# Single remainder chunks on GpSimd, expert products gathered by kind, a new hand-written order, and constant products in TensorE's early gaps

## The chip, the core and the metric

The kernel runs on one core of a Trainium2 chip. The metric is the device time of one execution in microseconds (us), lower is better. Engines are named TensorE (PE, its weight loads PEld), VectorE (DVE), ScalarE (ACT), GpSimd (POOL) and SyncE (SP), which issues most transfers.

## The reference

Attention restricted to hash buckets, then a small expert layer on 128 chosen tokens of each batch:

```python
q_bits = (np.einsum('bhsd,dk->bhsk', q, proj) > 0)      # B, H, S, D = 4, 8, 768, 64; 6 bits
mask = q_bucket[:, :, :, None] == k_bucket[:, :, None, :]
scores = np.where(mask, scale * np.matmul(q, k.T), -1e9)
attn = softmax(scores);  x = attn @ v                    # x: (4, 768, 512)
scores = np.einsum('bsd,d->bs', x, w_gate)
top_idx = np.argpartition(-scores[b], 128)[:128]         # per batch
ye = np.maximum(x[b, top_idx] @ w1, 0.0) @ w2            # 512 -> 1024 -> 512
out[b, top_idx] = x[b, top_idx] + sigmoid(scores[b, top_idx])[:, None] * ye
```

## The kernel before, in words

The 32 heads (4 batches of 8) are worked through one after the other, several of them in flight. Values are split into high and low parts so that products keep float32 accuracy.

Preparation of a head: its queries and keys are loaded (X), a product with the projection gives the hash (`hash_half`, hp), VectorE turns it into signs (`signs`, sg), ScalarE and VectorE make the high and low parts XH and XL (`split_xh`, `split_xl`), and SyncE moves signs and parts into the operand tiles A (four) and B (two) (`place_signs`, `place_a`, `place_b`).

Row maxima: the hash bits decide a row's maximum, up to a shift. For this GpSimd subtracts one half of A's keys from the other (`k_diff`, tile kd). For each of six row tiles t TensorE makes two products of 384 columns, one with kd and one with A's second half (`max_unit`, tile mx); ScalarE takes the positive part of the first (`max_relu`, tile me, 2 buffers), VectorE adds the second and reduces (`max_red`, mj and m). The six maxima are turned by a product (`max_turn`, mt), copied (mr) and moved into A by SyncE.

Scores: nine units a head, each a bank of 512 columns (`st_unit`, tile st, 3 buffers); ScalarE takes the exponential (`st_exp`, tile P). A chunk is 128 keys by 768 queries; six a head, in three pairs. The value product takes P's bfloat16 high part and a float16 remainder R = P − high part. The remainder of pair 1 (chunks 2 and 3) was one operation on GpSimd (`r_pair`), the other four chunks one operation each on VectorE (`r_chunk`). `av` then makes, for a chunk, six times three products of 65 or 64 columns; the third of three needs R. `recip` and `norm` divide and store x.

GpSimd and VectorE are kept apart by hand at some places: `mine` notes VectorE's last operation of the kind that reads two tiles of SBUF, and `turn` makes a GpSimd operation wait for it.

The expert layer: `score` sums x times the gate, `choose` ranks the tokens of a batch (compare: cm; count: rp; selection: sel; token numbers: ip, idx) and gathers the rows with an indirect transfer from GpSimd (xe). `expert` splits them into three parts (xth, xtl, xtb), multiplies by w1's high part (two products) and low part (one bfloat16 product), four k tiles and two halves e; the hidden values are turned (ht), split and multiplied by w2 in eight k tiles the same way (yp). `apply_expert` serves batches 0 and 1, `apply_expert_fast` batch 2, `apply_expert_last` batch 3. `warm_last` makes eight products of w1 into an unused bank (wp); `warm(n)` makes n products of a constant 128 by 128 tile into a score bank (ws).

The order of all work is a list of words, ORDER, run in sequence: `s.3.4` is score unit 4 of head 3, `rd.3.1` a max reduction, `c0` the next piece of `choose(0)`, `e1` the next piece of `apply_expert(1)`, `wu.30` is `warm(30)`. An engine does its own instructions in this order. BANKS names the PSUM bank (of four) of each max, hash and expert tile in turn.

Of the kernel before, what the change touches and what calls it, by code (L numbers as in the profile page):

```python
# [41 lines left out]
ps.0.1 sg.0.1.1.2 ps.0.0 V.0 lc xl.0 pb.0.2 h.0.1.2.4 sg.0.1.2.4 xh.1 pa.1.1 xh.2 xl.1 h.0.0.2.4 sg.0.0.2.4  # L42
h.0.0.1.2 sg.0.0.1.2 ps.1.0 ps.1.1 pa.1.0 pb.0.3 ir.0 mx.0.0.1 kd.0 mx.0.0.0 re.0.0 rd.0.0 mx.0.1.1 mx.0.1.0
re.0.1 mx.0.2.0 pb.0.1 rd.0.1 re.0.2 mx.0.2.1 rd.0.2 mx.0.3.0 mx.0.4.0 mc re.0.3 w mx.0.3.1 ir.1 rd.0.3 re.0.4
mx.0.5.0 mx.0.5.1 mx.0.4.1 kd.1 mx.1.0.0 rd.0.4 mx.1.1.0 vh.0 re.0.5 rd.0.5 pb.0.0 vl.0 mt.0 mx.1.0.1 re.1.0
rd.1.0 mc2.0 mr.0 pa.2.1 pa.2.0 re.1.1 mx.1.1.1 rd.1.1 mx.1.2.0 re.1.2 mx.1.2.1 ia.2 rd.1.2 mx.1.3.0 pb.1.1
mx.1.3.1 pb.1.2 ps.2.1 sv.0 re.1.3 mx.1.4.0 xh.3 ps.2.0 pa.3.0 pb.1.3 re.1.4 w mx.1.5.1 w w rd.1.3 xl.2 X.5
mx.1.4.1 rd.1.4 mx.1.5.0 re.1.5 s.0.3 ia.3 e.0.3 s.0.6 e.0.6 s.0.5 e.0.5 s.0.0 e.0.0 rd.1.5 mt.1 mc2.1 sh.0
mr.1 kd.2 s.0.1 e.0.1 sl.0 s.0.2 mx.2.0.1 e.0.2 r.0.1 s.0.7 e.0.7 r.0.0 mx.2.0.0 re.2.0 s.0.4 rd.2.0 pb.1.0
e.0.4 X.4 V.1 rr.0.1 mx.2.1.0 re.2.1 mx.2.1.1 mx.2.2.0 s.0.8 X.6 mx.2.3.0 re.2.2 mx.2.2.1 rd.2.1 rd.2.2  # L50
mx.2.4.0 s.1.3 e.0.8 pa.3.1 re.2.4 re.2.3 s.1.5 X.7 e.1.3 e.1.5 vh.1 pb.2.0 mx.2.5.0 s.1.6 mx.2.4.1 mx.2.5.1
mx.2.3.1 xl.3 a.0.0 a.0.1 ps.3.0 ps.3.1 a.0.2 rd.2.3 r.0.4 e.1.6 a.0.3 r.0.5 a.0.4 a.0.5 re.2.5 xh.6 xh.4
s.1.0 rd.2.4 rd.2.5 pb.2.1 rc.0 n.0.0 h.1.0.0.4 s.1.2 h.1.1.0.4 pb.2.2 w w n.0.2 e.1.0 e.1.2 mt.2 mc2.2 mr.2
n.0.1 s.1.1 e.1.1 s.1.4 pb.2.3 pa.4.1 mx.3.1.1 e.1.4 pa.4.0 vl.1 s.1.8 kd.3 mx.3.1.0 sg.1.0.0.4 re.3.1
sg.1.1.0.4 mx.3.0.0 mx.3.0.1 re.3.0 rr.1.1 r.1.0 r.1.1 s.1.7 mx.3.2.0 a.1.0 a.1.1 ps.4.1 pb.3.2 pb.3.3 V.2
rd.3.0 rd.3.1 e.1.7 mx.3.3.0 ps.5.0 e.1.8 r.1.5 w ps.4.0 r.1.4 re.3.3 w w mx.3.3.1 mx.3.2.1 s.2.0 re.3.2 s.2.3
e.2.0 e.2.3 mx.3.4.0 s.2.5 e.2.5 a.1.2 a.1.3 w xl.4 sv.1 a.1.4 rd.3.2 pb.3.1 a.1.5 rd.3.3 xh.5 pa.5.1 rc.1
sh.1 mx.3.5.0 re.3.4 mx.3.4.1 rd.3.4 s.2.1 re.3.5 kd.4 sl.1 n.1.2 n.1.1 mx.3.5.1 rd.3.5 s.2.2 pb.3.0 e.2.1
s.2.4 mx.4.1.0 ps.5.1 e.2.2 mt.3 mc2.3 xl.5 mx.4.1.1 r.2.0 e.2.4 X.9 mx.4.0.0 s.2.6 mr.3 r.2.1 pa.5.0 re.4.1
mx.4.3.0 s.2.7 s.2.8 pb.4.1 pa.6.0 pb.4.0 pa.6.1 mx.4.0.1 rr.2.1 re.4.0 rd.4.0 rd.4.1 n.1.0 mx.4.2.0 w a.2.0  # L60
e.2.6 e.2.8 re.4.2 a.2.1 mx.4.2.1 rd.4.2 mx.4.4.0 re.4.3 pb.4.3 mx.4.3.1 e.2.7 s.3.3 vh.2 rd.4.3 e.3.3 s.3.6
e.3.6 mx.4.4.1 a.2.2 a.2.3 r.2.4 vl.2 mx.4.5.0 re.4.4 kd.5 re.4.5 s.3.8 rd.4.4 mx.4.5.1 pb.4.2 rd.4.5 s.3.5
# [24 lines left out]
xh.12 a.7.5 pb.9.0 rd.9.5 mt.9 s.8.8 xl.11 mc2.9 mr.9 w r.8.1 e.8.8 mx.10.2.0 rc.7 n.7.0 mx.10.1.0 s.8.3 e.8.3
n.7.1 sv.4 s.8.5 s.8.7 e.8.5 r.8.0 s.8.4 pb.10.2 pb.10.3 mx.10.0.0 sh.4 e.8.7 re.10.0 s.9.3 n.7.2 c0 s.9.0
sl.4 re.10.1 mx.10.1.1 e.9.3 pb.10.0 e.8.4 mx.10.0.1 rr.8.1 a.8.0 a.8.1 s.9.1 c0 c0 mx.10.2.1 rd.10.0 e.9.0
# [152 lines left out]
def body(ctx, tc, qk, v, pj, wg, w1, w2, cst, out):  # L242
# [330 lines left out]
    def r_chunk(h, c):  # L573
# [4 lines left out]
        ))  # L578
        st["rd", h, c] = True

    def r_pair(h, g):
        need(*(("e", h, 3 * g + i) for i in range(3)))
        pp = st["P", h, g]
        turn(nc.gpsimd.tensor_tensor(  # L584
# [512 lines left out]
```

## Time and profile before

| what | value |
|---|---|
| median of 3 runs | 464.59 us (461.87 to 466.11) |
| the profiled execution | 464.73 us, its span 463.0 us |
| mean granted TensorE clock | 0.967 |
| ScalarE's busy time | 342.6 us |
| GpSimd's busy time | 170.6 us |

The span runs from the first to the last instruction of the profile. Rows of the timeline give start, duration, engine, line and the tiles written and read; in square brackets stands the idle time of the engine ahead of the row and what ended it. A group's row gives count, busy time, mean duration in ns, and idle time ahead of it.

### The profile page before, as it was taken

The numbers are of one execution on the slowest core, as the hardware profiler recorded it, in microseconds if no ns is written. First come the engines' busy times: TensorE is split into PE (matmuls) and PEld (weight loads), VectorE is DVE, ScalarE is ACT, GpSimd is POOL, SyncE is SP. The second block draws the span as 40 slices with busy tenths as digits, with TensorE's granted clock in tenths as the row PEclk, the third lists the DMA queues.
The fourth block names the chain that finished last, engine by engine and source line by source line (L and its number), as shares of the span: only waits on it lengthen the run. The fifth ranks groups of instructions, "written<-read, shape, count | busy, mean of one in ns | idle before, by whom it ended". The sixth has DMA issues, their size and how long they took to land. (4 is left out here: it accounts for less than half of the span.)

```text
span 463.0 us, 14030 instructions
## 1 busy us (share of the span) xinstructions
PE 435.8 (94%) x5443; PEld 351.0 (76%) x5453; DVE 370.3 (80%) x890; ACT 342.6 (74%) x826; POOL 170.6 (37%) x109
## 2 busy tenths in 40 slices
PE   7899999999889899999989999999999989999995
PEld 4576877878766788888868878798788878887663
DVE  4756978788878998887897998898999988767721
ACT  2687889989857788888478877888878857855431
POOL 4363645554243355331423433515333223224010
PEclk9589999999898999999999998999999989999999
DMA  6786878867756656565763845687646245400210
GB/s 215 207 230 169 227 217 230 217 190 212 212 178 168 178 124 184 171 170 133 211 174 102 212 130 172 167 197 212 197 122 183 73 112 124 138 2 25 69 47 23
DMA packets 33222, 73.17 MB, mean 158 GB/s; under 512 B 5298, under 2 KB 11652, under 8 KB 33156
## 3 DMA queue, kind: packets, MB, share of 16 engines
q1 hardware_dynamic: 21732, 52.70, 43.5%
q10 hardware_dynamic: 10592, 17.44, 12.5%
q0 software_dynamic: 832, 2.13, 1.5%
q8 instruction: 43, 0.70, 0.7%
q14 instruction: 23, 0.19, 0.1%
HBM read 25.84 MB, written 7.35 MB: 72 GB/s over the span
## 5 line engine op out<-in xcount | busy, mean ns | idle before, releaser
L584 POOL TENSOR_TENSOR R<-P 128x1536 f16<-128x1536 f32 x32 | 93.7, 2929 | 136.0 <-ACT P L559 45.5
L512 DVE CUSTOM_DVE_ANT_0 mj<-mx,me 128x384 bf16<-128x384 f32 x192 | 106.2, 553 | 39.4 <-ACT me L504 15.1
L541 PE MATMUL st<-A 97*128 97x256 f32 (+1 forms) x384 | 132.2, 358 | 4.2 <-DMA A<-mr 3.9
L576 DVE TENSOR_TENSOR R<-P 128x768 f16<-128x768 f32 x128 | 127.8, 1028 | 5.2 <-ACT P L561 3.2
L545 PE MATMUL st<-B 128*128 128x256 f32 (+1 forms) x384 | 128.1, 347 | 0.0
L559 ACT ACTIVATE P<-st 128x512 f32<-128x512 f32 x192 | 111.7, 606 | 15.5 <-PE st L545 9.4
L504 ACT ACTIVATE me<-mx 128x384 f32<-128x384 f32 x192 | 92.4, 495 | 36.7 <-PE mx L496 19.3
L609 PEld LDWEIGHTS <-P 128*128 128x128 bf16 x2304 | 112.3, 98 | 7.0 <-issue 3.4
L609 PE MATMUL av<-V,P 128*128 128x65 f16 (+1 forms) x2304 | 117.6, 195 | 0.0
L609 PE MATMUL av<-V,R 128*128 128x65 f16 x1152 | 114.4, 193 | 0.9 <-DVE R L576 0.4
L609 PEld LDWEIGHTS <-R 128*128 128x128 f16 x1152 | 107.3, 100 | 1.5 <-DVE R L576 1.0
L541 PEld LDWEIGHTS st<-A 97*128 97x128 f32 x384 | 74.7, 194 | 14.4 <-ACT x L633 2.8
L545 PEld LDWEIGHTS st<-B 128*128 128x128 f32 x384 | 75.0, 195 | 3.4
L496 PE MATMUL mx<-kd,A 96*128 96x384 f32 x192 | 68.4, 388 | 5.4 <-DVE m L512 2.8
L496 PE MATMUL mx<-A 96*128 96x384 f32 x192 | 66.8, 380 | 2.6 <-DVE XL L387 1.8
L487 POOL TENSOR_TENSOR kd<-A 96x384 fp32r<-96x384 f32 x32 | 35.3, 1104 | 89.6 <-PE mx L496 28.5
L561 ACT ACTIVATE P<-st 128x512 f32<-128x512 f32 x96 | 57.4, 604 | 3.1 <-PE st L545 2.4
L633 ACT ACTIVATE x<-av,rc 128x64 f32<-128x64 f32 x192 | 46.5, 323 | 11.6 <-DVE rc L621 7.8
L496 PEld LDWEIGHTS mx<-kd,A 96*128 96x128 f32 x192 | 36.9, 199 | 16.3 <-DVE m L512 5.7
L496 PEld LDWEIGHTS mx<-A 96*128 96x128 f32 x192 | 37.8, 200 | 11.6 <-DVE XL L387 2.5
L387 DVE SCALAR_TENSOR_TENSOR XL<-X,XH 128x768 fp32r<-128x768 f32 x32 | 31.1, 971 | 0.3 <-issue 0.2
L382 ACT ACTIVATE XH<-X 128x768 fp32r<-128x768 f32 x32 | 27.0, 849 | 5.3 <-DMA A<-XH 5.2
(106 smaller groups left out, 449.9 us busy)
## 6 DMA issues: line engine op xcount, KB each, us to landing
A<-XH SPq DMA_DIRECT2D x64, 192.0 KB
B<-XL SPq DMA_DIRECT2D x64, 192.0 KB
B<-A SPq DMA_DIRECT2D x64, 192.0 KB
X<-in_qk_dram SPq DMA_DIRECT2D x31, 384.0 KB
V<-in_v_dram ACTq DMA_DIRECT2D x16, 384.0 KB
out_dram<-x ACTq DMA_DIRECT2D x8, 768.0 KB
W<-in_w_dram ACTq DMA_DIRECT2D x8, 512.0 KB
A<-sg SPq DMA_DIRECT2D x64, 18.0 KB
```

The source lines that it names most:

```text
L487: turn(nc.gpsimd.tensor_tensor(kd, a[0:96, 1, 0:384].bitcast(F32), a[0:96, 1, 384:768].bitcast(F32), op=ALU.subtract))
L496: nc.tensor.matmul(pt[:, :384], a[0:96, 0, t * P : (t + 1) * P], a[0:96, 1, 384:768] if i else st["kd", h], start=True, stop=True,)
L504: nc.scalar.activation(me, st["mx", h, t, 0][:, :384], AF.Relu)
L512: nc.vector.tensor_tensor_reduce(out=jk[:, :384], in0=st["mx", h, t, 1][:, :384], in1=st["me", h, t], op0=ALU.add, op1=ALU.max, scale=1.0, ...
L541: nc.tensor.matmul(pt[:, o : o + n], a[:, 1, c * P : (c + 1) * P], a[:, 0, q0 : q0 + n], start=True, stop=False,)
L545: nc.tensor.matmul(pt[:, o : o + n], bt[:, 1, c * P : (c + 1) * P], bt[:, 0, q0 : q0 + n], start=False, stop=True,)
L559: nc.scalar.activation(pp[:, r, 0:512], pt, AF.Exp, scale=ES)
L561: nc.scalar.activation(pp[:, :, 512:768], pt.rearrange("p (a b) -> p a b", a=2), AF.Exp, scale=ES)
L576: mine(nc.vector.tensor_tensor(r_tile(h, c // 2)[:, r], pp[:, r], hi_view(pp, r), op=ALU.subtract))
L584: turn(nc.gpsimd.tensor_tensor(r_tile(h, g), pp, pp.bitcast(BF16)[:, :, 1::2], op=ALU.subtract))
L609: nc.tensor.matmul(o[:, t, 0:n], l, vv[:, c, hh, v0 : v0 + n], start=False, stop=last and l is lo, skip_group_check=True,)
L633: nc.scalar.activation(x[:, t], o[:, t, 0:D], AF.Copy, scale=rc[:, t : t + 1])
```

## The change

Six things change together.

- Remainders: each chunk is an operation of its own, by the order list either on VectorE (`r_dve`, word r, 91 of them where 128 were) or on GpSimd (`r_pool`, word g, 101 where 32 pairs were).
- kd: on GpSimd (`kd_pool`, 18 heads) or on VectorE (`kd_dve`, word kv, 14 heads).
- The me tiles have three buffers where they had two.
- Expert products: the two products with a high part of the weights are made for each k, and the bfloat16 products with the low part are gathered, four in a row. In the last expert the parts of the second half are put in another sequence.
- Constant products: besides `wu.30` at the start there are twelve more such words (4, 8, 35, 46, 2, 3, 5, 2, 5, 2, 5 and 8 products, 125 in all), up to the first scores.
- ORDER and BANKS are new throughout.

```diff
+ME = 3
...
-X.1 X.0 X.2 X.3 i0 ia.0 ia.1 wu.30 h.0.0.0.1 h.0.1.1.2 xh.0 pa.0.1 pa.0.0 h.0.1.0.1 sg.0.0.0.1 sg.0.1.0.1
+i0 wu.30 X.1 xh.1 wu.4 h.0.0.1.2 h.0.1.1.2 X.0 X.3 X.2 lc ia.0 wu.8 h.0.0.0.1 sg.0.0.0.1 sg.0.0.1.2 h.0.1.0.1
...
-        kd = sb.tile([96, 384], F32R, tag="kd", name=f"kd{h}", bufs=1)
-        turn(nc.gpsimd.tensor_tensor(
-            kd, a[0:96, 1, 0:384].bitcast(F32), a[0:96, 1, 384:768].bitcast(F32), op=ALU.subtract
-        ))
...
+    def kd_pool(h):
+        turn(nc.gpsimd.tensor_tensor(**k_diff(h)))
+
+    def kd_dve(h):
+        mine(nc.vector.tensor_tensor(**k_diff(h)))
...
-        me = sb.tile([P, 384], F32, tag="me", name=f"me{h}_{t}", bufs=2)
+        me = sb.tile([P, 384], F32, tag="me", name=f"me{h}_{t}", bufs=ME)
...
-    def r_pair(h, g):
-        need(*(("e", h, 3 * g + i) for i in range(3)))
-        pp = st["P", h, g]
-        turn(nc.gpsimd.tensor_tensor(
-            r_tile(h, g), pp, pp.bitcast(BF16)[:, :, 1::2], op=ALU.subtract
-        ))
...
+    def rest(h, c):
         need(("e", h, 3 * (c // 2) + 2), ("e", h, 3 * (c // 2) + c % 2))
...
+    def r_dve(h, c):
+        mine(nc.vector.tensor_tensor(**rest(h, c)))
+
+    def r_pool(h, c):
+        turn(nc.gpsimd.tensor_tensor(**rest(h, c)))
...
+    def two(ks):
+        return [(k, i) for k in ks for i in (0, 1)]
+
+    def lows(ks):
+        return [(k, 2) for k in ks]
...
-                m.up(hp, e, (k,))
+                m.up(hp, e, two((k,)))
                 yield
+            m.up(hp, e, lows(range(4)))
+            yield
...
-        m.up(h1, 1, range(2), (0, 2, 1), True)
+        m.up(h1, 1, by_part(range(2), (0, 1, 2)))
...
-        m.up(h1, 1, range(2, 4), (0, 2, 1), True)
+        m.up(h1, 1, by_part(range(2, 4), (2, 0, 1)))
```

Three places show how instructions move. First TensorE's list between the last hash product of the first heads and the first max products; before:

```order
L358 MATMUL hp_0_2_180<-X_103,pjt 32x384
L358 MATMUL hp_0_1_184<-X_97,pjt 32x384
L496 MATMUL mx_0_1_193<-A_83 128x384
L496 MATMUL mx_0_0_197<-kd_195,A_83 128x384
L496 MATMUL mx_1_1_204<-A_83 128x384
```

and with the change (the first dots stand for the rest of 46 constant products, the second for one more):

```order
L362 MATMUL hp_1_2_228<-X_147,pjt 32x384
L307 LDWEIGHTS ones_75
L307 MATMUL ws_246<-ones_75 128x128
...
L505 MATMUL mx_0_0_293<-kd_244,A_83 128x384
L505 MATMUL mx_0_1_302<-A_83 128x384
L505 MATMUL mx_1_0_304<-kd_244,A_83 128x384
L505 MATMUL mx_3_0_310<-kd_244,A_83 128x384
L307 LDWEIGHTS ones_75
...
L505 MATMUL mx_1_1_317<-A_83 128x384
```

Constant products now stand ahead of the max products and among them, and the first max product is one with kd. Second GpSimd's list around heads 16 and 17 (R_0, R_1, R_2 are the three pairs of a head); before:

```order
L487 TENSOR_TENSOR kd_4440<-A_84 96x384
L584 TENSOR_TENSOR R_1_4474<-P_1_4383 128x1536
L487 TENSOR_TENSOR kd_4544<-A_85 96x384
L857 DMA out_dram<-ye_4546,idx_3350 3072x512
L584 TENSOR_TENSOR R_1_4892<-P_1_4742 128x1536
```

and with the change:

```order
L496 TENSOR_TENSOR kd_4719<-A_85 96x384
L592 TENSOR_TENSOR R_0_4899<-P_0_4700 128x768 x2
L592 TENSOR_TENSOR R_1_4970<-P_1_4897 128x768 x2
L592 TENSOR_TENSOR R_2_5051<-P_2_4985 128x768
L592 TENSOR_TENSOR R_0_5127<-P_0_5008 128x768 x2
L592 TENSOR_TENSOR R_1_5157<-P_1_5154 128x768
L592 TENSOR_TENSOR R_2_5211<-P_2_5017 128x768 x2
```

Where one pair stood for a head, five singles of head 16 (rows two to four) follow one another, some of them as a couple of one tile (x2); there are 20 such couples in the whole list, and at other heads fewer singles stand between two kd. Third TensorE's list where the rows of the last expert are turned (xp); before:

```order
L849 MATMUL yp_9077<-w2l,htb_8978 128x512
L777 MATMUL xp_9104<-cs,xe_9074 128x128 x4
L849 MATMUL yp_9077<-w2h,hth_8977 128x512
L849 MATMUL yp_9077<-w2h,B_87 128x512
L849 LDWEIGHTS htb_8978
L849 MATMUL yp_9077<-w2l,htb_8978 128x512
```

and with the change:

```order
L852 LDWEIGHTS htb_9145
L852 MATMUL yp_9188<-w2l,htb_9145 128x512
L782 MATMUL xp_9273<-cs,xe_9247 128x128 x4
L814 MATMUL mh_0_9289<-w1h,xth_9278 128x512 x4
L814 LDWEIGHTS xtb_9280
L814 MATMUL mh_0_9289<-w1l,xtb_9280 128x512
```

Before, six products of batch 2's expert stood behind the turned rows; now all of them stand ahead. The eight products of `warm_last` stood among the counts of batch 3 and are now TensorE's last.

More of the change, by code (lines that the diff above doesn't have):

```diff
@@ L46 @@
[L46 to L50, printed above, removed]
@@ L803, in gate2, with up @@
             nc.vector.reciprocal(ss[:, 1:2], ss[:, 1:2])
-        def up(hp, e, ks, order=(0, 1, 2), by_part=False):
-            ki = [(k, i) for k in ks for i in order]
-            if by_part:
-                ki = [(k, i) for i in order for k in ks]
-            for k, i in ki:
+        def up(hp, e, kis):
+            done = t.get(("u", e), 0)
+            for k, i in kis:
                 l, r = t["x"][i]
@@ L812, in up @@
                     hp, l[:, k * P : (k + 1) * P], r[:, k, e * 512 : e * 512 + 512],
-                    start=(k == 0 and i == order[0]), stop=(k == 3 and i == order[-1]),
+                    start=done == 0, stop=done == 11,
                 )
+                done += 1
+            t["u", e] = done
         def relu(hp, e):
@@ L841, in split_h2, with down @@
             nc.vector.tensor_tensor(hl[:, f], tp, hh[:, f].bitcast(F32), op=ALU.subtract)
-        def down(yp, ks, order=(0, 1, 2), by_part=False):
-            ki = [(k, i) for k in ks for i in order]
-            if by_part:
-                ki = [(k, i) for i in order for k in ks]
-            for k, i in ki:
+        def down(yp, kis):
+            done = t.get("d", 0)
+            for k, i in kis:
                 l, r = t["h"][i]
@@ L850, in down @@
                     yp, l[:, k * P : (k + 1) * P], r[:, k],
-                    start=(k == 0 and i == order[0]), stop=(k == 7 and i == order[-1]),
+                    start=done == 0, stop=done == 23,
                 )
+                done += 1
+            t["d"] = done
         def finish(yp):
@@ L883, in st_bank, with by_part @@
         return pst.tile([P, 512], F32, tag="st", name=name)
+    def two(ks):
+        return [(k, i) for k in ks for i in (0, 1)]
+    def lows(ks):
+        return [(k, 2) for k in ks]
+    def by_part(ks, order=(0, 2, 1)):
+        return [(k, i) for i in order for k in ks]
     def apply_expert(b):
@@ L910, in apply_expert @@
         for k in range(8):
-            m.down(yp, (k,))
+            m.down(yp, two((k,)))
             yield
+            if k % 4 == 3:
+                m.down(yp, lows(range(k - 3, k + 1)))
+                yield
         yield
@@ L924, in apply_expert_fast @@
         for k in range(4):
-            m.up(h0, 0, (k,))
+            m.up(h0, 0, two((k,)))
             yield
+        m.up(h0, 0, lows(range(4)))
+        yield
         m.relu(h0, 0)
@@ L929, in apply_expert_fast @@
         for k in range(2):
-            m.up(h1, 1, (k,))
+            m.up(h1, 1, two((k,)))
             yield
@@ L937, in apply_expert_fast @@
         for k in range(2, 4):
-            m.up(h1, 1, (k,))
+            m.up(h1, 1, two((k,)))
             yield
+        m.up(h1, 1, lows(range(4)))
+        yield
         m.relu(h1, 1)
@@ L942, in apply_expert_fast @@
         for k in range(2):
-            m.down(yp, (k,))
+            m.down(yp, two((k,)))
             yield
@@ L949, in apply_expert_fast @@
         for k in range(2, 8):
-            m.down(yp, (k,))
+            if k == 4:
+                m.down(yp, lows(range(4)))
+                yield
+            m.down(yp, two((k,)))
             yield
+        m.down(yp, lows(range(4, 8)))
+        yield
         m.finish(yp)
```

371 lines of the change are left out of this document (189 added, 182 removed), and 10 rows, old and new, of the table BANKS.

## The prediction

> **What bounds the kernel now.** First the page: its shares of busy time, and the row of the granted clock.
>
> ```profile
> span 463.0 us, 14030 instructions
> PE 435.8 (94%) x5443; PEld 351.0 (76%) x5453; DVE 370.3 (80%) x890; ACT 342.6 (74%) x826; POOL 170.6 (37%) x109
> PEclk9589999999898999999999998999999989999999
> ```
>
> TensorE is the engine to follow, VectorE the next. The clock row dips in its second and third slice and in a few later ones. The view by stretches shows the start, the body and two of the later dips:
>
> ```profile
> 0.00:11.70 11.70, 8.20 (x46) 4.67 (x46) 5.57 (x9) 3.39 (x4) 5.33 (x14) 1.00 0.66 215
> 12.33:25.98 13.65, 12.75 (x43) 8.60 (x44) 9.32 (x31) 9.22 (x19) 6.11 (x9) 0.50 0.76 193
> 26.00:427.00 401.00, 384.56 (x5177) 318.03 (x5183) 340.09 (x804) 318.43 (x780) 155.54 (x85) 0.98 0.61 164
> 138.60:142.00 3.40, 3.40 (x19) 1.45 (x21) 2.37 (x4) 3.23 (x10) 1.61 (x1) 0.50 0.19 40
> 374.10:377.50 3.40, 3.40 (x70) 3.40 (x67) 3.17 (x7) 1.93 (x4) 1.00 (x1) 0.51 0.73 205
> ```
>
> (Columns: length, then TensorE, its weight loads, VectorE, ScalarE, GpSimd, then the granted clock, DMA share and GB/s.) At the start TensorE runs at half clock for 13.65 us. Five short stretches of the body look like the last two rows.
>
> A busy TensorE is not one at its peak. The starts of its products in the timeline show how dense they can stand:
>
> ```profile
> 409.26 0.28 PE L541 MATMUL st<-A 97*128 97x256 f32 x1
> 409.38 0.28 PE L545 MATMUL st<-B 128*128 128x256 f32 x1
> 409.50 0.34 PE L496 MATMUL mx<-kd,A 96*128 96x384 f32 x1
> 409.68 0.34 PE L496 MATMUL mx<-A 96*128 96x384 f32 x1
> 409.86 0.39 PE L849 MATMUL yp<-w2h,hth 128*128 128x512 f32 x1
> 410.09 0.40 PE L849 MATMUL yp<-w2h,htl 128*128 128x512 f32 x1
> 426.05 0.22 PE L609 MATMUL av<-V,P 128*128 128x65 f16 x2
> 426.14 0.22 PE L609 MATMUL av<-V,P 128*128 128x65 f16 x2
> ```
>
> A 256-column product takes 0.12 us, 384 columns 0.18, 512 columns 0.23, and three value products 0.09. By the code there are 768 score products (half of 512 columns, half of 256), 384 max products and 3456 value products; they need 134, 69 and 104 us so, together 307. The experts' 192 products add 44. With hashes, sums and transposes I estimate 390 us of the 463. So some 70 us are waits and lost clock, and those a new order can reach. What the waits are, these rows show:
>
> ```profile
> 272.92 2.75 POOL L584 TENSOR_TENSOR R<-P 128x1536 f16<-128x1536 f32 x1 [2.90 <-ACT P L559]
> 273.25 2.79 DVE L740 TENSOR_SCALAR sel<-iota,rank 128x128 f16<-128x128 f16 x3
> 276.57 0.67 PE L745 MATMUL ip<-tok,sel 128*128 128x1 f16 x6 [1.07 <-DVE m L512]
> 133.77 1.07 POOL L487 TENSOR_TENSOR kd<-A 96x384 fp32r<-96x384 f32 x1 [3.61 <-PE mx L496]
> 133.89 3.02 DVE L576 TENSOR_TENSOR R<-P 128x768 f16<-128x768 f32 x1
> 134.81 1.28 POOL L670 TENSOR_TENSOR w2l<-W,w2h 128x512 bf16<-128x512 f32 x1
> 138.38 0.22 PE L521 MATMUL mt<-identr,m 128*6 128x128 f32 x1 [2.24 <-DVE m L512]
> 368.81 2.71 DVE L740 TENSOR_SCALAR sel<-iota,rank 128x128 f16<-128x128 f16 x3
> ```
>
> While GpSimd works on its pair of chunks (272.92 to 275.67), VectorE's small sel operations stretch to 2.79 us: the two engines exclude each other. Behind them wait the max reductions, TensorE's max banks stay full, and TensorE idles 1.07 us. At 133.89 a chunk on VectorE takes 3.02 us, through two GpSimd operations in a row, and TensorE idles 2.24 us. There are five holds of over 2 us (the first at 133.89, the last at 368.81), and after four of them follows one of the half-clock stretches.
>
> **The change part by part.** The prices of one operation, from the views of the lines and the page's groups:
>
> ```profile
> L576 DVE TENSOR_TENSOR R<-P x128: 917/952/3020, 28.7 to 425.6; 128x768 f16<-128x768 f32 x128
> L584 POOL TENSOR_TENSOR R<-P x32: 2746/2843/3333, 30.6 to 421.5; 128x1536 f16<-128x1536 f32 x32
> L487 POOL TENSOR_TENSOR kd<-A x32: 989/1012/1823, 11.6 to 392.7; 96x384 fp32r<-96x384 f32 x32
> L670 POOL TENSOR_TENSOR w1l<-W,w1h x8: 1277/1286/1874, 23.7 to 83.1; 128x512 bf16<-128x512 f32 x8
> L375 DVE TENSOR_SCALAR sg<-hp 128x384 fp32r<-128x384 f32 x14 | 7.3, 550 | 0.2 <-PE hp L358 0.2
> ```
>
> *The start.* Here stand what TensorE's 30 constant products took, the hash products (two records each, so 8 in 4.82 us) and the first max product:
>
> ```profile
> 1.01 3.38 PE L303 MATMUL ws<-ones 128*128 128x128 f16 x30 [1.01 <-POOL ones L284]
> 5.07 4.82 PE L358 MATMUL hp<-X,pjt 128*32 128x384 f32 x16 [0.68 <-DMA X<-in_qk_dram]
> 11.74 0.41 PE L496 MATMUL mx<-A 96*128 96x384 f32 x1 [1.84 <-DVE XL L387]
> ```
>
> Added are 125 such products, 93 ahead of the first max product and 32 between the max products of heads 0 and 1. At 0.11 us each (3.38 over 30) the 93 cost 10 us, at twice that rate 5; idle TensorE time before 11.7 us is 3.5 (11.70 less 8.20). They are not wholly covered. Head 1's two hash products (0.6 each) and twelve of the constants also come ahead of head 0's hash, so head 0's signs, which SyncE moves, land about 2.3 us later (1.2 and some 1.1). I therefore set the first max product 2.3 us later, with the last block of 46 just filling the wait. Its kd now comes from VectorE (0.55 there, by the sg row of as many elements, against 1.0 on GpSimd). That is a new wait on VectorE for the moved signs; behind it queue the XL of head 0 and the first max reductions, which free TensorE's max banks and the me buffers. In return the clock should stay full: it fell at 12.33, behind the idle 1.84, which now holds products. At full clock TensorE's 12.75 us in that stretch shrink to about 6.4 and VectorE's 9.32 bind, which saves 13.65 − 9.3 = 4.3. Net −2.0. Ends: −4.3 if nothing is late; +5.8 if the clock falls all the same and the 32 cost 3.5 more.
>
> *Single chunks.* VectorE loses 37 of 128 chunks (37 × 0.952 = 35.2 us) and gains 14 kd (14 × 0.55 = 7.7): 27.5 us less. GpSimd gets 101 singles for 32 pairs and 18 kd for 32. No row has a single: it is at least half a pair, 1.37, and at most 1.93 (the 512-element w1l by 768/512). I take 1.45, near half the pair, since operation and types are the same. GpSimd then works 146 on chunks against 93.7, in all near 210 of 463, still with room. A hold lasts at most 1.45 us instead of 2.75, unless singles stand in a row, and 20 couples do (rows with x2). Five holds cost 5 × 1.65 us idle (the mean of 1.07 and 2.24) and four half-clock stretches 4 × 1.7 (half of 3.4): 15.1 us. I take half of it: −7.5. Ends: −15.1, and +12 if four more holds come than go.
>
> *New order, a third buffer for me.* The waits view names the couple which a third buffer loosens:
>
> ```profile
> DVE mj L512 <- ACT me L504: 15.1, 24, 2.8
> ACT me L504 <- DVE m L512: 14.6, 16, 2.5
> ```
>
> These are idle times of VectorE and ScalarE, and only their trace in TensorE counts. In the body TensorE idles 401 − 384.6 = 16.4 us by the stretch row, part of it already in the holds. With VectorE 27.5 us lighter I take a quarter: −4.0. Ends: −16.4 (all), and +8 (half the idle time of now once more), where value products wait for a chunk that GpSimd does late. A single waits for its own chunk's exponentials and for VectorE's last operation on the shared side, no longer for the whole pair; but on GpSimd's queue it stands behind earlier singles, kd and the weights' low parts, and the gathers of the experts' rows stand behind it. SyncE's list keeps its 329 rows; only their order moves.
>
> *Gathered expert products.*
>
> ```profile
> 410.79 0.40 PE L849 MATMUL yp<-w2h,htl 128*128 128x512 f32 x1
> 445.50 1.28 PE L811 MATMUL mh<-w1h,xth 128*128 128x512 f32 x4
> 448.41 0.62 PE L811 MATMUL mh<-w1h,xth 128*128 128x512 f32 x2
> ```
>
> Mixed by threes, a period is 410.09 to 410.79: 0.233 each. Gathered, as the last expert has it already, twelve take 445.50 to 448.41: 0.243 each. I take 0, with ends −1.0 and +1.5 for 144 products.
>
> *The tail.*
>
> ```profile
> 439.72 0.97 POOL L755 DMA_INDIRECT xe<-out_dram,idx x1 [13.17 <-DVE idx L1031]
> 444.50 0.59 ACT L784 CAST xth<-xp 128x512 fp32r<-128x512 f32 x1 [2.04 <-PE xp L777]
> ```
>
> The last expert waits for its gather (439.72) and then for xth, ready at 445.09; its products start at 445.50 behind six of the expert before. These now come earlier, and the eight warming products move from ahead of them to the very end, beside the closing transfer: −0.4, ends −0.4 and +1.3 (the six not done in time).
>
> Sum: −2.0 − 7.5 − 4.0 + 0 − 0.4 = −13.9. The profiled execution took 464.73 us, 1.7 beyond its span and 0.14 over the median of the runs (464.59): 464.7 − 13.9 = **450.8 us**.
>
> **The rivals.** *Holds by chains (slower).* The row at 133.89 shows a hold through two GpSimd operations. With the 20 couples, and up to five of six chunks of heads 16 and 17 on GpSimd, holds near 2.9 us can become more frequent than the five of now. Each costs 3.0 (15.1 / 5). Against −6.4 from the other terms, nine such holds make it slower: 464.7 − 6.4 + 4 × 3.0 = 470.3; with ten 473.3. Against it: most singles stand apart.
>
> *Holds vanish (faster still).* If a held VectorE operation goes in as soon as the running GpSimd operation ends, no hold exceeds 1.45 us and all 15.1 go; with 12 of the 16.4 us of idle: 464.7 − 2.0 − 15.1 − 12 − 0.4 = 435.2. The row at 133.89 speaks against it, the pairs (one operation, one hold) leave it open. The Trainium skill, page "SBUF — State Buffer", section "SBUF: two separate sides", says that the shared port pair is locked for one whole instruction and that the loser blocks fully; by that the holds end with each single. The trace agrees for the pair at 272.92 (held until 275.67) and not for the two at 133.77 and 134.81.
>
> *Nothing moves.* The order before already hides VectorE, and the holds only change places: A start of −2.0 and −0.4 leave 462.3. For it: TensorE's floor of 390 us does not move at all.
>
> **How the numbers follow.** Forecast 0.48 (442 to 459), holds vanish 0.21, nothing moves 0.17, chains 0.14. A measurement of this kernel tells about 1% (4.6 us) from no change. Faster by over 1% are the first two, 0.69; within 1% 0.17; slower 0.14. The range runs from 437, inside the second case, to 468, which leaves out the worse chains: 437 to 468. The ends of the terms together (427 and over 490) are wider, but would need all to fall one way.
>
> **What would show it.** Right: a granted clock of 1.00 from 12 to 26 us and first scores before 24 us; VectorE near 340 us busy, GpSimd near 210; a single at 1.4 to 1.5 us; no VectorE chunk above 2.4 us; at most two half-clock stretches in the body. Wrong: chunks held 2.9 us behind couples of singles, idle TensorE before value products with GpSimd's R as releaser, or a first max product after 15 us.

## The result, and the profile after

The changed kernel took 466.32 us (median of 20 runs, 463.49 to 471.42), the kernel before 461.96 beside it (20 runs, 459.14 to 469.24): a ratio of 1.0101, 95% interval 1.0069 to 1.0132. It is slower by 1.0%, some 4.4 us; forecast were 13.9 us less. Ratios, here and below, compare each kernel's faster executions alone, so that they can differ from the ratio of two medians. The profiled execution of the changed kernel took 465.07 us; that of before, 464.73, lies 2.8 us above the median that 20 runs give, which is why the two spans hardly differ.

From the page of the changed kernel: the span, the busy times, the granted clock, GpSimd's chunks.

```profile
span 463.2 us, 14366 instructions
PE 439.2 (95%) x5578; PEld 357.6 (77%) x5578; DVE 353.7 (76%) x867; ACT 344.2 (74%) x826; POOL 221.6 (48%) x164
PEclk9999999999999997999998999999989999999999
L592 POOL TENSOR_TENSOR R<-P 128x768 f16<-128x768 f32 x101 | 159.6, 1593 | 136.7 <-DVE R L589 40.9
```

And its stretches, cut as in the prediction:

```profile
0.00:11.70 11.70, 10.70 (x89) 7.10 (x91) 4.37 (x7) 2.97 (x3) 7.79 (x18) 1.00 0.81 254
12.33:25.98 13.65, 13.06 (x121) 9.15 (x119) 10.08 (x32) 8.83 (x18) 5.83 (x6) 1.00 0.51 132
26.00:427.00 401.00, 383.40 (x5157) 319.20 (x5155) 323.48 (x783) 321.31 (x781) 203.49 (x136) 0.98 0.63 166
```

The clock stays at 1.00 through the start, as meant, and VectorE is 16.6 us lighter. Neither shortens the kernel: in the body TensorE is busy 383.4 us of 401, where it was 384.6. What the start gives to the first max product is seen in the timelines, here the kernel before (SyncE's move of head 0's signs, GpSimd's kd, ScalarE's load of the first weights) and then the changed kernel:

```profile
8.42 1.57 SPq L394 DMA_DIRECT2D A<-sg  x2
11.64 0.99 POOL L487 TENSOR_TENSOR kd<-A 96x384 fp32r<-96x384 f32 x1 [5.52 <-DVE XL L387]
15.64 0.36 ACTq L657 DMA_DIRECT2D W<-in_w_dram  x1
```

```profile
6.01 0.46 ACTq L662 DMA_DIRECT2D W<-in_w_dram  x1
8.57 2.17 DVE L379 TENSOR_SCALAR sg<-hp 32x384 fp32r<-32x384 f32 x4 [6.08 <-PE hp L362]
10.77 2.88 SPq L398 DMA_DIRECT2D A<-sg  x3
15.04 0.55 DVE L499 TENSOR_TENSOR kd<-A 96x384 fp32r<-96x384 f32 x1 [1.19 <-DMA A<-sg]
15.65 0.45 PE L505 MATMUL mx<-kd,A 96*128 96x384 f32 x1 [0.32 <-DVE kd L499]
```

The signs leave 2.4 us later and then need 4.3 us to land instead of at most 3.2; the first max product comes at 15.65 instead of 11.74. Of these 3.9 us, 1.8 are left at the first scores (25.46 instead of 23.64). The holds of the body have other faces than before. Two places of the changed kernel (score sums jks, GpSimd's chunks, TensorE's max products):

```profile
238.98 3.89 POOL L592 TENSOR_TENSOR R<-P 128x768 f16<-128x768 f32 x2 [2.79 <-ACT P L570]
239.71 1.83 DVE L652 CUSTOM_DVE_ANT_0 jks<-x,wgt 128x512 bf16<-128x512 f32 x1
241.58 1.83 DVE L652 CUSTOM_DVE_ANT_0 jks<-x,wgt 128x512 bf16<-128x512 f32 x1
244.81 0.44 PE L505 MATMUL mx<-kd,A 96*128 96x384 f32 x1 [1.82 <-DVE sg L379]
...
338.66 1.01 POOL L496 TENSOR_TENSOR kd<-A 96x384 fp32r<-96x384 f32 x1 [5.21 <-PE mx L505]
338.76 2.89 DVE L652 CUSTOM_DVE_ANT_0 jks<-x,wgt 128x512 bf16<-128x512 f32 x1
339.63 1.46 POOL L592 TENSOR_TENSOR R<-P 128x768 f16<-128x768 f32 x1
```

A score sum takes 0.69 when nothing is in its way. The group's mean, before and after:

```profile
L647 DVE CUSTOM_DVE_ANT_0 jks<-x,wgt 128x512 bf16<-128x512 f32 x18 | 13.1, 728 | 1.8
```

```profile
L652 DVE CUSTOM_DVE_ANT_0 jks<-x,wgt 128x512 bf16<-128x512 f32 x18 | 18.5, 1026 | 1.6
```

Over all operations of VectorE that a GpSimd operation overlapped, the time beyond the usual one of their form (its first quartile, where the excess is over 0.1 us) adds to some 25 us before and some 32 after. Holds of over 2 us beyond the usual time fell from five to two (61.65 and 338.76); the smaller ones became more.

### The profile page after: what moved, and what is told of

Its sections match the earlier page's. It is cut to its first block, busy times and chain, and to the rows that moved or that the text cites. A ratio compares the mean times of both kernels' runs of the same rounds, so it can differ in the third digit from the quotient of the medians.

```text
span 463.2 us, 14366 instructions
## 1 busy us (share of the span) xinstructions
PE 439.2 (95%) x5578; PEld 357.6 (77%) x5578; DVE 353.7 (76%) x867; ACT 344.2 (74%) x826; POOL 221.6 (48%) x164
## 5 line engine op out<-in xcount | busy, mean ns | idle before, releaser
L592 POOL TENSOR_TENSOR R<-P 128x768 f16<-128x768 f32 x101 | 159.6, 1593 | 136.7 <-DVE R L589 40.9
L550 PE MATMUL st<-A 97*128 97x256 f32 (+1 forms) x384 | 130.4, 354 | 2.9 <-DMA A<-mr 2.9
L554 PE MATMUL st<-B 128*128 128x256 f32 (+1 forms) x384 | 126.2, 344 | 0.0
L614 PE MATMUL av<-V,P 128*128 128x65 f16 (+1 forms) x2304 | 120.1, 195 | 0.0
L614 PE MATMUL av<-V,R 128*128 128x65 f16 x1152 | 116.2, 193 | 0.7 <-POOL R L592 0.2
L589 DVE TENSOR_TENSOR R<-P 128x768 f16<-128x768 f32 x91 | 94.0, 1055 | 6.0 <-ACT P L570 4.0
L505 PE MATMUL mx<-kd,A 96*128 96x384 f32 x192 | 64.3, 366 | 4.3 <-DVE m L521 1.9
L505 PEld LDWEIGHTS mx<-A 96*128 96x128 f32 x192 | 36.1, 193 | 10.5 <-DVE m L521 4.3
L496 POOL TENSOR_TENSOR kd<-A 96x384 fp32r<-96x384 f32 x18 | 20.1, 1116 | 44.9 <-PE mx L505 12.2
L391 DVE SCALAR_TENSOR_TENSOR XL<-X,XH 128x768 fp32r<-128x768 f32 x32 | 34.6, 1084 | 1.5 <-ACT XH L386 1.5
```

Of the source, the lines that this page charges most:

```text
L391: mine(nc.vector.scalar_tensor_tensor(xl, st["X", h], XS, st["XH", h].bitcast(F32), op0=ALU.mult, op1=ALU.subtract))
L505: nc.tensor.matmul(pt[:, :384], a[0:96, 0, t * P : (t + 1) * P], a[0:96, 1, 384:768] if i else st["kd", h], start=True, stop=True,)
L550: nc.tensor.matmul(pt[:, o : o + n], a[:, 1, c * P : (c + 1) * P], a[:, 0, q0 : q0 + n], start=True, stop=False,)
L554: nc.tensor.matmul(pt[:, o : o + n], bt[:, 1, c * P : (c + 1) * P], bt[:, 0, q0 : q0 + n], start=False, stop=True,)
L589: mine(nc.vector.tensor_tensor(**rest(h, c)))
L592: turn(nc.gpsimd.tensor_tensor(**rest(h, c)))
```

## The experiments

Each line: median of 6 to 12 executions, and ratio to the kernel before run beside it on the same chip, with its 95% interval. The kernel before took 462.2 to 463.7 in these.

| run | what | median us | ratio to before |
|---|---|---|---|
| a_nowu | changed, without the 125 added products | 466.49 | 1.0115 (1.0065 to 1.0164) |
| a_start | changed, start of before | 462.18 | 1.0011 (0.9974 to 1.0048) |
| b_start | before, changed start | 466.86 | 1.0091 (1.0048 to 1.0134) |
| b_split | before, pairs as two singles | 460.37 | 0.9973 (0.9932 to 1.0015) |
| a_sg | changed, head 0's signs first | 468.93 | 1.0148 (1.0089 to 1.0207) |
| a_e0late | changed, first expert's start later | 466.03 | 1.0099 (1.0064 to 1.0133) |
| a_sel | changed, sel and jks in the hand-made order | 455.31 | 0.9882 (0.9822 to 0.9942) |
| b_me3gath | before, third me buffer, gathered products | 462.26 | 1.0004 (0.9966 to 1.0042) |
| a_w | changed, first weights' load late | 465.99 | 1.0069 (1.0032 to 1.0106) |
| a_w_lc | the same, constants late too | 468.66 | 1.0112 (1.0060 to 1.0164) |
| a_w_sel | a_w and a_sel | 454.15 | 0.9818 (0.9771 to 0.9866) |
| b_sel | before, sel and jks in the hand-made order | 456.62 | 0.9874 (0.9833 to 0.9916) |
| a_sg_w | a_sg and a_w | 464.78 | 1.0055 (1.0010 to 1.0099) |
| a_start_sel | a_start and a_sel | 453.48 | 0.9848 (0.9781 to 0.9915) |
| b_split_sel | b_split and b_sel | 459.89 | 0.9969 (0.9929 to 1.0010) |
| a_jks | a_sel with jks alone | 459.33 | 0.9896 (0.9818 to 0.9975) |
| a_all | a_sel, a_sg and a_w | 452.59 | 0.9785 (0.9733 to 0.9837) |
| a_all_gather | a_all, first gather let through | 450.21 | 0.9732 (0.9672 to 0.9791) |

### Start and body apart

The order is a list of words, so one kernel's first words can stand in front of the other's rest. b_start takes the changed order up to its last `wu` word (116 words) and then the words of before that are still missing; a_start the first 97 words of before and then the rest of the changed ones. BANKS follows its tiles. a_nowu only drops words; b_split splits the pair:

```diff
-        turn(nc.gpsimd.tensor_tensor(
-            r_tile(h, g), pp, pp.bitcast(BF16)[:, :, 1::2], op=ALU.subtract
-        ))
+        for r in range(2):
+            turn(nc.gpsimd.tensor_tensor(
+                r_tile(h, g)[:, r], pp[:, r], hi_view(pp, r), op=ALU.subtract
+            ))
```

> The changed kernel without the 125 added constant products (only the first 30 stay); nothing else differs. Theory 'start': the added products keep the granted clock at 1.00 from 12 to 26 us, but the first max product moved from 11.74 to 15.65 us, and that delay is paid to the end; without them the first max product comes before 14 us again, the clock dips to about 0.5 somewhere before 26 us, and the time is 2 to 4 us below the changed kernel's (near 463). Theory 'holds': the loss lies in the body, where GpSimd's singles hold VectorE for 31.8 us in all against 24.7 before; then the time stays within 1 us of the changed kernel's 466.3, or rises by the half clock.

> The changed kernel with the order of before for its first 97 words (hashes, signs and max products of heads 0 and 1 up to the end of the added products, kd of head 0 on GpSimd, no added products), and its own order from there. Theory 'start': the first max product near 11.7 us, half clock from 12 to 26 us as before, first scores near 23.6, and the time 2 to 4 us below the changed kernel's 466.3. Theory 'holds': within 1 us of 466.3.

> The kernel before with the first 116 words of the changed order (all added constant products, kd of head 0 on VectorE), and its own order behind them. Theory 'start': 2 to 4 us slower than before (464 to 466). Theory 'holds', with my forecast's term for the start: 1 to 3 us faster than before (459 to 461), with the clock at 1.00 from 12 to 26 us.

> The kernel before with each of its 32 pairs on GpSimd as two single chunks in a row at the same place; nothing else differs. A single takes 1.46 us by the changed kernel's rows, two of them 2.9 where the pair took 2.75. Theory 'holds': what holds VectorE is the time GpSimd works, not the length of one operation, so VectorE's operations are held as long as before or longer and the time is the same or up to 3 us more (462 to 465). My forecast's term: a held operation goes in between the two singles, no hold is over 1.5 us, and the time falls by 3 us or more (below 459). Theory 'start' says nothing of it.

a_start and b_start agree: the start alone costs 4 us, the whole loss, and the rest of the change nothing that can be told. The added products are not to blame: without them (a_nowu) the time is the same and the first max product still late, at 15.31 us, now with half clock. In b_start the clock did not stay full, it fell to half for 3.4 us at 19.7 and again at 26.5 us. In b_split neither theory is shown, the time is within the interval of no change. Its trace shows why so little comes of the singles where the selections stand; here GpSimd's pair, VectorE's sel and TensorE's max products in the kernel before, and then the same place with two singles in b_split:

```profile
157.71 2.75 POOL L584 TENSOR_TENSOR R<-P 128x1536 f16<-128x1536 f32 x1 [5.10 <-ACT P L559]
158.13 2.71 DVE L740 TENSOR_SCALAR sel<-iota,rank 128x128 f16<-128x128 f16 x3
161.37 0.62 PE L496 MATMUL mx<-kd,A 96*128 96x384 f32 x2 [1.16 <-DVE m L512]
```

```profile
156.07 2.89 POOL L585 TENSOR_TENSOR R<-P 128x768 f16<-128x768 f32 x2 [5.09 <-ACT P L559]
156.49 2.69 DVE L741 TENSOR_SCALAR sel<-iota,rank 128x128 f16<-128x128 f16 x3
159.71 0.61 PE L496 MATMUL mx<-kd,A 96*128 96x384 f32 x2 [1.05 <-DVE m L512]
```

The first sel (1.10 us) ends when the first single does, at 157.5, and the second (1.50 us) when the second does, at 159.0. By the pair three sel took 2.71 us and TensorE idled 1.16; with two singles it is 2.69 and 1.05. The Trainium skill, page "SBUF — State Buffer", section "SBUF: two separate sides", says that the engine which starts first has the shared ports for its whole instruction and the other is blocked. Here the trace agrees, but between two singles only one small operation goes in, and the next single holds the next one, so the sum stays what GpSimd works.

### The start

Words moved (a_sg: head 1's hash and signs behind head 0's; a_w: the first `w`; a_w_lc: also `lc` and `mc`):

```diff
-wu.4 h.0.0.1.2 h.0.1.1.2 X.0 X.3 X.2 lc ia.0 wu.8 h.0.0.0.1 sg.0.0.0.1 sg.0.0.1.2 h.0.1.0.1
+wu.4 X.0 X.3 X.2 lc ia.0 wu.8 h.0.0.0.1 sg.0.0.0.1 h.0.1.0.1 h.0.0.1.2 h.0.1.1.2
-xh.0 pa.0.1 ir.1 sg.0.1.1.2 pa.0.0 sg.0.1.0.1 ps.0.1 ia.1 ps.0.0 wu.35
+xh.0 pa.0.1 ir.1 sg.0.1.0.1 pa.0.0 ps.0.1 ia.1 ps.0.0 sg.0.0.1.2 sg.0.1.1.2 wu.35
```

```diff
-ps.1.0 sg.0.1.2.4 pa.1.0 w mc pb.0.0 kv.0 wu.46
+ps.1.0 sg.0.1.2.4 pa.1.0 mc pb.0.0 kv.0 wu.46
-mx.0.4.0 re.0.3 re.0.2
+mx.0.4.0 re.0.3 w re.0.2
```

> The changed kernel with one thing reordered in the start: head 0's two hash products and its signs come ahead of head 1's on TensorE, VectorE and in SyncE's list (as in the kernel before); the 125 added products, their places and kd on VectorE stay. Theory 'signs': what costs the start 4 us is that head 0's signs leave 2.4 us later (10.77 us instead of 8.42) because head 1's are made ahead of them; then here the first max product comes at 13 to 14 us instead of 15.65, and the time falls by 1.5 to 3.5 us (463 to 465), with the clock still at 1.00. Rival 'products in the way': TensorE, filled by the added products, is late itself; then the first max product stays after 15 us and the time at 466.

> The changed kernel with its first word w (ScalarE's queue then issues the 512 KB load of the first weights at 6.01 us) moved behind the fourth max step of head 0, where the kernel before has it (issued at 15.64); nothing else differs. Theory 'transfers': head 0's signs are small, but they land late because of the large transfers issued ahead of them: 3.2 us from issue (8.42) to GpSimd's kd (11.64) before, 4.3 us in the changed kernel (10.77 to 15.04), 6.2 without the added products (8.50 to 14.70) and 7.9 with head 0's signs first (8.49 to 16.44), so that making the signs earlier did not help. With the load late, kd starts 2 to 3 us earlier, the first max product comes before 14 us, and the time falls by 2 to 4 us (462 to 464). Rival 'SyncE's list': the signs wait for SyncE's own transfers (X, constants, XH); then nothing changes (466).

> As the run before, with the 259.5 KB load of the constants (lc, issued by SyncE at 2.61 us, 10.03 in the kernel before) and the copies made of it (mc) moved to the places of before too. Theory 'transfers': a further 0.5 to 1.5 us earlier than with the weights alone, first max product at 12 to 13 us, 461 to 463. Rival 'SyncE's list': the whole gain comes only here, 3 to 4 us below the changed kernel, and none in the run before.

> The changed kernel with both edits of the start: head 0's hash and signs ahead of head 1's, and the first weights' load late. Alone the first made it slower (signs issued at 8.49 us but landed at 16.44) and the second gained 1.6 us by its trace (signs issued at 10.05, kd at 13.04 with no wait). Theory 'two delays in a row' (signs made late, and transfers in their way, each hiding the other): kd near 11.5 us, first max product at 12 to 13, first scores near 22.5, 2 to 4 us below the changed kernel (462 to 464). Rival: the queue of transfers is full anyway (V, the constants, X of heads 2 and 3), and the signs land after 14 us again: no faster than with the late load alone (466).

My theory of the signs fell with a_sg, which was not faster (468.93). Its move of the signs and its kd, then those of a_w and of a_sg_w:

```profile
8.49 2.35 SPq L398 DMA_DIRECT2D A<-sg  x3
16.44 0.55 DVE L499 TENSOR_TENSOR kd<-A 96x384 fp32r<-96x384 f32 x1 [4.30 <-DMA A<-sg]
```

```profile
10.05 2.52 SPq L398 DMA_DIRECT2D A<-sg  x3
13.04 0.55 DVE L499 TENSOR_TENSOR kd<-A 96x384 fp32r<-96x384 f32 x1
```

```profile
8.31 2.99 SPq L398 DMA_DIRECT2D A<-sg  x3
12.29 0.55 DVE L499 TENSOR_TENSOR kd<-A 96x384 fp32r<-96x384 f32 x1
```

In a_sg the signs leave 2.3 us earlier than in the changed kernel and land 1.4 later: issued 2.5 us behind the 512 KB of weights (5.97 there), they take 7.9 us. TensorE stands 3.4 us for them, and half clock comes back for 13.65 us (from 16.7). With the weights late, kd has no wait for the signs: they land within 3.0 us in a_w and 4.0 in a_sg_w. So two delays stood in a row: the first max product comes at 14.41 in a_w and 13.66 in a_sg_w, the first scores at 24.19 and 23.44 (25.46 in the changed kernel). The gain, by the ratios some 1.5 and 2 us, is short of what I expected or at its low end, and not clear of the noise: the intervals overlap that of the changed kernel. About half of the 4 us of the start stays open: the move of before was issued at 7.27 in a_start, and head 0's hash began at 5.13 where a_sg_w has 5.59.

a_w_lc is not faster than a_w, against both theories; by the medians it is 2.7 us slower, though the intervals overlap. VectorE's copies of the constants now stand among the first max reductions, where GpSimd works:

```profile
16.57 1.00 POOL L496 TENSOR_TENSOR kd<-A 96x384 fp32r<-96x384 f32 x1 [7.63 <-DVE m L521]
16.60 1.06 DVE L323 CAST iota<-cs 128x128 f16<-128x128 f32 x1
17.52 1.45 POOL L294 MEMSET A<- 32x1536 f32 x1
17.58 1.42 DVE L324 CAST tok<-cs 128x6 f16<-128x6 f32 x1
```

Copies of 0.22 and 0.17 us take 1.06 and 1.42: a hold again, through a subtraction and a memset, and half clock behind it (18.7 to 25.5).

### The held small operations

R, XL and cm stood in `mine` (and kd, where VectorE makes it), sel and jks did not, although jks reads two tiles of SBUF. a_sel, b_sel and the runs built on them wrap both; a_jks has the second hunk only:

```diff
-            nc.vector.tensor_scalar(sel[:, t], iota16, rank[:, t : t + 1], None, op0=ALU.is_equal)
+            mine(nc.vector.tensor_scalar(sel[:, t], iota16, rank[:, t : t + 1], None, op0=ALU.is_equal))
-            nc.vector.tensor_tensor_reduce(
+            mine(nc.vector.tensor_tensor_reduce(
                 out=jk[:, : d1 - d0], in0=x[:, t, d0:d1], in1=wgt[:, d0:d1],
...
-            )
+            ))
```

> The changed kernel in which VectorE's selections and score sums (sel, jks) also count for the hand-made order of the two engines: a GpSimd operation that stands behind them in the list waits until they are done. Nothing else differs. Theory 'holds': the held small operations (sel 1.2 us each, jks up to 2.2 us) cost TensorE some 1 to 2 us each, about 10 us over the ranking stretches; with fewer of them held the time falls by 2 us or more (464 or less). Rival 'holds are cheap': GpSimd's chunk only starts later and value products wait for it instead; within 1 us of 466.3, or slower.

> The changed kernel with only jks (the score sums) in the hand-made order, sel as it was. By the traces, heads 16 and 24, where jks stood held (three of 1.1 to 2.2 us at 239.71, 241.58 and 338.76), gained 7.6 of the 10.6 us, and the stretch at 279, where sel was held, some 1.3. Theory 'jks first': 456 to 459. Rival 'sel first' (sel stands in the chain of ranking, gather and expert): 461 or more.

> The kernel before (pairs on GpSimd, its own order) with sel and jks in the hand-made order of the two engines. Theory 'holds': the pairs' holds of sel (2.1 to 2.2 us at 158.13, 273.25 and 368.81) go, with the half-clock stretches behind them, 4 to 9 us faster than before (454 to 459), so what I expected of the single chunks was to be had from the order of the two engines alone. Rival: a pair that waits for the selections is late for its value products; within 2 us of before.

> The kernel before with its pairs as two single chunks each, and sel and jks in the hand-made order. With pairs that order gave 456.6; two sel holds of 2.1 and 2.3 us were left (152.90, 265.57), where the pair stood ahead of sel in the list. If single chunks are worth something once the small operations are kept apart, as my forecast of the holds had it, these two holds shrink and the time is 2 us or more below 456.6. Rival: two singles in a row hold as long as a pair; within 1.5 us of 456.6.

> The kernel before with three buffers for me instead of two, and with the gathered expert products in batches 0 to 2; order and all else as before. My forecast gave the gathered products nothing and the third buffer a share of 4 us together with the new order. Theory 'the max stage is not the bound': within 1 us of before. Rival: the third buffer alone loosens the waits of VectorE and ScalarE on each other (15.1 and 14.6 us idle), 2 us or more faster than before.

a_sel is 11 us faster than the changed kernel (10 by the ratios), far more than I expected. The same place as above, in a_sel, and the stretch from 236 to 249.5 us in the changed kernel and in a_sel:

```profile
238.97 0.69 DVE L652 CUSTOM_DVE_ANT_0 jks<-x,wgt 128x512 bf16<-128x512 f32 x1
239.81 3.48 POOL L592 TENSOR_TENSOR R<-P 128x768 f16<-128x768 f32 x2 [5.10 <-DVE sc L652]
```

```profile
236.00:249.50 13.50, 11.68 (x112) 9.28 (x112) 12.09 (x27) 9.99 (x23) 5.91 (x5) 0.87 0.54 151
```

```profile
236.00:249.50 13.50, 13.43 (x182) 11.30 (x179) 10.30 (x29) 12.05 (x30) 8.73 (x6) 1.00 0.55 160
```

GpSimd waits 5.10 us for the last score sum, all six of which take 0.69, and nothing waits for its chunk: TensorE fills the stretch, at full clock. By the ends of the heads' value products in the two traces, 1.7 us are won by head 12 (sel), 3.4 at head 16 (the score sums above), 1.3 by head 20 (sel) and 4.2 at head 24 (score sums). Held time fell from some 32 to 24 us. a_jks alone gets some 7 of the 11 us by the medians and 9 of the 10 by the ratios, and its interval holds a_sel's 0.9882: the score sums are most of it, and that the selections count too is seen in the traces only. V's split, not kept apart either, was held for 3.49 us in the kernel before (236.26); no run wraps it.

b_sel shows that the stake was there before the change, and needed none of it: 1.3% from two wrapped calls. The gain, some 5.8 us, lies within the 4 to 9 expected. b_split_sel is not faster than b_sel but slower, 0.9969 against 0.9874: the singles are not worth anything once jks is kept apart, and its sel are held as in b_split (by 1.04 and 1.26 us at 271). Held time is some 3 us longer than in b_sel; whether that is its whole loss is not shown. Buffers and gathered products (b_me3gath) give nothing that can be told, as expected.

### The first gather

a_e0late moves the first two `e0` words behind `mx.14.0.1` and `n.11.1`. a_all_gather moves `rd.13.0 rd.13.1` from behind `a.11.3` to ahead of `r.11.2`.

> The changed kernel with the first two pieces of the first expert (its transposes, gate and splits) moved some 30 words later, behind two products of head 14's maxima; nothing else differs. In the changed kernel the gather of its rows took 4.57 us on GpSimd (163.73 to 168.30, where 1.48 before), while VectorE ran kd, R, V and two R in a row from 163.37 to 167.38; TensorE then stood 3.5 us at 171.33 and ran at half clock for 6.8 us (3.3 us lost). Theory 'gather': that stall is a loss of the new order; with the pieces later the stall of 3.5 us goes, and with it most of the half clock: 3 to 6 us faster than the changed kernel (460 to 463). Rival: only the place of the wait changes, since ScalarE and VectorE have other work that was late there; within 1.5 us of 466.3.

> The changed kernel with the three edits that gained: sel and jks in the hand-made order of the two engines, head 0's hash and signs ahead of head 1's, and the first weights' load late. Theory 'the losses are independent': 455.3 (order of the engines alone) less the start's 1.5 to 3, so 452 to 454, and faster than both given kernels by 1.5% or more. Rival: the start's gain is eaten by later waits, 455 to 456.

> As the run before, with the first two max reductions of head 13 moved on VectorE between the split of V and the two R that follow it. In every run with the changed order the first gather of rows took 4.57 us on GpSimd (1.48 to 1.50 in the runs with the order of before), ending 1.0 us after VectorE's row of kd, R, V, R, R. Theory 'the row of VectorE holds the gather': with the max reductions in the row the gather ends within 2 to 3 us, TensorE's stall of 3.5 us behind it shrinks by 1.5 us or more, and the time is 1.5 to 4 us below the run before. Rival: the gather is slow for itself (its first use); it stays at 4.57 us, and the time is the same or up to 1 us more.

> The start of before in front of the changed order, with sel and jks in the hand-made order of the two engines. Alone the two gave 4.1 and 11 us below the changed kernel's 466.3. Theory 'the losses are independent': 450 to 452.5. Rival: part of the one hides behind the other, 454 to 456.

> The changed kernel with the first weights' load late and with sel and jks in the hand-made order of the two engines. If the two findings are independent, both gains add: 455.3 less 2 to 4, so 451 to 453. If the late start was hidden by the waits that the second edit took away, it stays near 455.

First the kernel before (VectorE's one chunk beside GpSimd's gather):

```profile
166.13 0.95 DVE L576 TENSOR_TENSOR R<-P 128x768 f16<-128x768 f32 x1
166.50 1.48 POOL L755 DMA_INDIRECT xe<-out_dram,idx  x1 [1.13 <-DVE idx L750]
```

then the changed kernel (GpSimd's gather, VectorE around it, TensorE's transposes of the gathered rows):

```profile
163.37 0.54 DVE L499 TENSOR_TENSOR kd<-A 96x384 fp32r<-96x384 f32 x1
163.73 4.57 POOL L760 DMA_INDIRECT xe<-out_dram,idx  x1 [2.04 <-DVE idx L755]
163.84 0.95 DVE L589 TENSOR_TENSOR R<-P 128x768 f16<-128x768 f32 x1
164.71 0.94 DVE L440 SCALAR_TENSOR_TENSOR V<-V,V 128x768 f16<-128x768 f32 x1
165.57 1.81 DVE L589 TENSOR_TENSOR R<-P 128x768 f16<-128x768 f32 x2
167.31 0.55 DVE L521 CUSTOM_DVE_ANT_0 mj<-mx,me 128x384 bf16<-128x384 f32 x1
174.95 1.09 PE L782 MATMUL xp<-cs,xe 128*128 128x128 f32 x4 [3.34 <-DMA xe<-out_dram,idx]
```

and in a_all_gather:

```profile
162.39 2.92 POOL L760 DMA_INDIRECT xe<-out_dram,idx  x1 [0.36 <-DVE idx L755]
163.45 0.95 DVE L440 SCALAR_TENSOR_TENSOR V<-V,V 128x768 f16<-128x768 f32 x1
165.83 0.56 DVE L521 CUSTOM_DVE_ANT_0 mj<-mx,me 128x384 bf16<-128x384 f32 x1 [1.43 <-ACT me L513]
166.91 1.82 DVE L589 TENSOR_TENSOR R<-P 128x768 f16<-128x768 f32 x2
172.50 0.60 PE L782 MATMUL xp<-cs,xe 128*128 128x128 f32 x4
```

The gather ends 0.9 us after VectorE's row of two-input operations does, in all three. With the row cut it takes 2.92 us, the stall is gone, and no half clock follows: by the traces 4.8 us are won against a_all between the ends of heads 10 and 12, by the medians the kernel is 2.4 us faster. The theory holds for the gather and the stall; the time is of the size expected, but the intervals of the two runs overlap. The Trainium skill, page "DMA: Bandwidth & Descriptors", section "SWDGE vs HWDGE vs iDMA", says that the descriptors which GpSimd makes lie in SBUF, and that VectorE locks it out of writing them during its 2-port perf mode. The trace agrees that VectorE's row holds the gather; whether these operations run in that mode no run here shows. a_e0late only moved the stall: TensorE idled 3.19 us ahead of 182.89, at the expert's first product. By its trace 2.0 us were won between heads 8 and 29, by the medians nothing.

Whether the gains add is not settled. a_all came where it was expected. a_w_sel lies 1 us below a_sel by the medians and 3 by the ratios, where 2 to 4 were expected; a_start_sel lies about 2 us below, less than the 4 of its start. The intervals of both overlap a_sel's. a_all_gather is the best version: 450.21 us, 2.7% faster than the kernel before (ratio 0.9732, 0.9672 to 0.9791) and faster than the changed one. It also lies below b_sel (0.9874, 0.9833 to 0.9916): with its own losses mended, the changed kernel has some 1.4% that the two wrapped calls alone do not give.

## Why the prediction was wrong

Between the forecast, −13.9 us, and the measured +4.4 lie 18.3 us: 6.2 in the start, 6.3 in the single chunks, 4.0 in the term of order and buffer, and 1.8 that no run places.

**The start (−2.0 forecast, +4.2 by b_start).** The step that failed is "head 0's signs, which SyncE moves, land about 2.3 us later", and the saving of 4.3 us set against it. The order of hashes and signs cost the 2.4 us that I counted at their issue; landing cost more, and a_w points to the load of the first weights, which ScalarE issues and which had moved from 15.64 to 6.01 us. I counted the words of SyncE's list and not the transfer on the other queue. My sign of being wrong, a first max product after 15 us, came (15.65). The clock came as forecast, 1.00 throughout the start, but the 24 max products of the two heads went from 11.4 to 9.6 us (first to last start), 1.9 saved instead of 4.3. That ScalarE and VectorE, busy 8.4 and 7.6 us of that time, set their pace is likely and not shown. The two together make +2.0 (3.9 later, 1.9 saved), near the 1.8 at the first scores; the other half of the 4.2 stays open. It is not a plain delay that is passed on: by the traces head 0's value products end 0.3 us later in the changed kernel than in a_start, head 6's 1.6 and head 16's 2.4. a_nowu shows the clock and the added products to be worth nothing together.

**Single chunks (−7.5 forecast; −1.2 by b_split, −3.1 to +0.7).** The step "a hold lasts at most 1.45 us instead of 2.75" took a hold for the length of one GpSimd operation, with couples of singles as the one exception. By b_split's rows each GpSimd operation that starts across a row of small VectorE operations holds one of them anew. There are 101 starts instead of 32, GpSimd works 66 us more on chunks (159.6 against 93.7), and held time rose although the holds of over 2 us fell from five to two. My sign "no VectorE chunk above 2.4 us" failed at 61.65 us, where an R took 3.88 through kd and two w1l. The half-clock stretches of the body fell from five of 3.4 us to three, one of them of 6.8, not to two. Of the 15.1 us that I had at stake, the order of the engines won 5.8 in the kernel before (b_sel). b_split moves no chunk away from VectorE; what the 37 moved chunks are worth alone no run measures.

**Order, buffer, lighter VectorE (−4.0 forecast).** b_me3gath: nothing for the buffer. a_start against b_split, 462.18 and 460.37, leaves nothing for the order either, as long as sel, jks and the gather are held in it. The cover failed: VectorE is 16.6 us lighter in the body and TensorE as busy as before, and what gained was to keep held operations free (a_sel, b_sel). VectorE came to 353.7 us, not 340: the row of jks alone grew by 5.4 us.

**Gathered products (0) and tail (−0.4).** Right in kind: 1.0004, and from the last value product to the last scatter 30.7 us against 31.7.

**The base.** The sum was made against an execution that lay 2.8 us above the median of 20 runs; its three runs did not show it.

**The rivals.** "Holds by chains" had the sign and part of the mechanism, but in the wrong place (sel and jks, not couples of singles among chunks), and the start, which decided the sign, had no rival of its own. The range of 437 to 468 us holds the measured time only at its far end, put there for the chains of holds and not for a slower start: that it lies inside is luck.

## What to carry to other kernels

Where two engines exclude each other, look first at what the small operations in a row cost that are not kept apart, before cutting the large ones: two calls wrapped in the order of the engines gave 1.3%, and the whole rearrangement, as it stood, lost 1.0%. When a load moves to an earlier place on another queue, look for the small transfer behind it that somebody waits for. An order that is written as a list can be cut in two and joined with another's: two such runs say in which part a loss lies.

## What the runs showed of the hardware

- VectorE holds GpSimd as well: a gather took 4.57 us on GpSimd during a row of kd, R, V, R, R, 2.92 with the row cut after V, 1.48 to 1.50 in the orders of before, with one R beside it. Each time it ended 0.9 us after VectorE's last operation of that row.
- Casts of 128 by 128 elements, 0.22 us alone, took 1.06 to 1.41 during a GpSimd subtraction and a memset.
- An 18 KB move took 7.9 us when it was issued 2.5 us behind 512 KB on another queue (a_sg), and at most 4.0 when those came later (a_sg_w).
- The granted clock fell to half not only after idle time: in the 3.4 us ahead of each such stretch TensorE was still busy for 1.2 to 2.3 us in the kernel before and 0.9 to 1.6 in the changed one.
